# Attention in compact chunks whose scores contract over one head's 64 rows, with whole loads of queries and paired half loads on two queues

## The chip, the cores and the metric

The kernel runs on one core of one Trainium2 chip. The metric is the device time of one execution in microseconds (us), as the median of several runs; less is better. TensorE is called PE below, its weight loads PEld, VectorE DVE, ScalarE ACT, GpSimd POOL and SyncE SP.

## What is computed

Attention over 2 batches, 8 heads, 576 positions, 64 elements a head (float32). Heads 0 to 3 see a local window of 32 positions, heads 4 to 7 every 32nd position. Its result, as 1152 tokens of 512, goes through two products and a gated one, and then through four experts.

```python
stride = 32
scale = 1.0 / np.sqrt(D)
scores = scale * np.matmul(q, k.transpose(0, 1, 3, 2))
rel = pos[:, None] - pos[None, :]
mask_local = (rel >= 0) & (rel < stride)
mask_strided = (rel >= 0) & (pos[None, :] % stride == pos[:, None] % stride)
# masked scores, softmax over the keys, and the sum over v
x = attn_out.transpose(0, 2, 1, 3).reshape(B * S, H * D)   # 1152 x 512
a, b = x @ w1, x @ w2                                       # 512 -> 1024
x = ((a * b) @ w3) @ w_out                                  # 1024 -> 1024 -> 512
# four experts: out += p[:, e] * (relu(x @ w1[e]) @ w2[e])
```

## The kernel before

Attention output is kept as two float32r parts, `x_hi` and `x_lo` (value and remainder), and every large product is three matmuls of such parts (`mm3`). The float64 weights come as 1 MB loads (`raw`, two buffers) and are turned into the two parts by a chain of elementwise steps for each 128x1024 chunk: `round_up` (L121, ACT), `magnitude` (L127 DVE for the first chunk, L129 ACT for the others), `clamp` (L132), `shift` (L135), `sign` (L138) and `add` (L142) on DVE, then `split_hi` (L149, ACT) and `split_lo` (L159, DVE). A generator, `work()`, holds these steps for all chunks in one order; `advance(n)` issues the next n of them, and `need(c)` issues steps until chunk c is ready. `add` also issues the load of the raw chunk after next. A chunk is split only while `live`, the count of 128x1024 buffers in use (16 in all), is at most 14.

Attention runs in 22 tiles, 11 a batch: six of 96 queries for the four local heads, five of 126 or 108 for the strided ones (there queries are laid out by residue, 18 positions each). A tile takes: a mask matmul and four score matmuls into one bank (L285, L288; the queries of the other head of a pair are zeros, so that 128 rows are contracted), the maxima and their scaling (DVE, L294, L296), four exponentials with sums (ACT, L303), the division (DVE, L309, L310, L312), four transposes (L318), their evacuation in halves by ACT and DVE (L323), four value matmuls (L331), and `x_hi` (ACT, L345) and `x_lo` (DVE, L348).

The order is the program's own: every engine runs its instructions as the Python code issued them. The main loop is a pipeline over the tiles: step s holds the scores of tile s, the division of tile s-1, the transposes of tile s-3 and the values of tile s-4. From step 15 on, when the first batch (b = 0) is through, each step also issues one unit, `ab_block` (L232 to L234): 24 matmuls of 288 columns for one of 8 weight chunks `w12`, one batch and one half of its positions. There are 32 units, 16 of each batch. Units 2k and 2k+1 use chunk k, and batch 0's come first; chunk k's buffers come free with unit 17 + 2k. After unit 31 come `wc_tile` (`wc_acc`), `x3_block` and the experts; they are not touched by the change.

SP's queue carries nearly all loads in the order they are issued in; ACT's queue carries one. A DMA takes the next of eight semaphores (`DMAHW0` to `DMAHW7`) and waits until the DMA that held it before has landed; the wait stands in the program of the engine that issues it.

## Time and profile before

| | |
|---|---|
| median of 3 runs | 647.94 us (647.41 to 649.07) |
| the profiled execution, its time | 648.42 us |
| its span, first to last instruction | 646.6 us |
| PE / PEld / DVE / ACT busy, share of the span | 97% / 89% / 73% / 45% |
| first unit's first matmul | 48.57 us |
| first `wc` matmul, after all units | 167.83 us |

The span falls into three parts: attention of batch 0 up to 48.6 us, the units with what is left of attention up to 167.8 us, and the untouched rest. Busy shares are to be read stage by stage: PE's 97% holds long stretches at 100% and a start at about 75%. In the trace a float32 matmul stands as two passes (x8 is four matmuls), each with a weight load; the duration of a pass includes its way through the array, so the pace is read from start to start.

### The profile page before, as it was taken

The numbers are of one execution on the slowest core, as the hardware profiler recorded it, in microseconds if no ns is written. First come the engines' busy times: TensorE is split into PE (matmuls) and PEld (weight loads), VectorE is DVE, ScalarE is ACT, GpSimd is POOL, SyncE is SP. The second block draws the span as 40 slices with busy tenths as digits, with TensorE's granted clock in tenths as the row PEclk, the third lists the DMA queues.
The fourth block names the chain that finished last, engine by engine and source line by source line (L and its number), as shares of the span: only waits on it lengthen the run. The fifth ranks groups of instructions, "written<-read, shape, count | busy, mean of one in ns | idle before, by whom it ended". The sixth has DMA issues, their size and how long they took to land.

```text
span 646.6 us, 10360 instructions
## 1 busy us (share of the span) xinstructions
PE 629.1 (97%) x4052; PEld 572.7 (89%) x4052; DVE 470.6 (73%) x888; ACT 291.7 (45%) x628; POOL 6.9 (1%) x18
## 2 busy tenths in 40 slices
PE   7769999999999999999999999999999999999998
PEld 6659989999888999988999889988788989899896
DVE  8899999599875423777887787787776566665743
ACT  6787776466554323343333343344433333333321
POOL 4000000000000000000000000000000000000000
PEclk9989999999999999999999999999999999999999
DMA  8943133134433310234353355334478474656311
GB/s 227 308 133 131 66 131 131 67 131 143 183 131 130 131 66 1 67 131 188 137 188 138 134 192 183 142 131 163 163 260 322 151 247 153 228 177 239 130 66 66
DMA packets 26385, 98.73 MB, mean 153 GB/s; under 512 B 2528, under 2 KB 3808, under 8 KB 23776
## 3 DMA queue, kind: packets, MB, share of 16 engines
q1 hardware_dynamic: 26192, 97.97, 43.5%
q8 instruction: 32, 0.52, 0.4%
q14 instruction: 17, 0.14, 0.1%
q10 hardware_dynamic: 144, 0.10, 0.1%
HBM read 78.92 MB, written 19.14 MB: 152 GB/s over the span
## 4 chain that ended last, share of the span: by engine, by line
PE 85%; DVE 8%; DMA 3%; ACT 2%; SPq 1%; issue 1%; DVEq 0%
PE g_acc L233 10%; PE g_acc L234 10%; PE g_acc L232 10%; PE ab_acc L232 5%; PE ab_acc L234 4%; PE ab_acc L233 4%; PE m_a L232 4%; PE m_a L234 4%; PE m_a L233 4%; PE x_acc L232 3%; PE x_acc L233 3%; PE x_acc L234 3%; PE m_b L234 3%; PE m_c L232 3%; PE m_c L233 3%; PE m_c L234 3%
## 5 line engine op out<-in xcount | busy, mean ns | idle before, releaser
L517 ACT ACTIVATE h_hi<-u 128x320 fp32r<-128x320 f32 (+1 forms) x128 | 56.9, 445 | 189.2 <-DVE u L523 189.2
L233 PE MATMUL g_acc<-w_lo,h_hi 128*128 128x512 f32 (+1 forms) x296 | 114.9, 388 | 0.0
L232 PE MATMUL g_acc<-w_hi,h_hi 128*128 128x512 f32 (+1 forms) x296 | 114.7, 387 | 0.0
L234 PE MATMUL g_acc<-w_hi,h_lo 128*128 128x512 f32 (+1 forms) x296 | 114.6, 387 | 0.0
L523 DVE TENSOR_TENSOR u<-m_b,u 128x320 f32<-128x320 f32 (+1 forms) x96 | 40.8, 453 | 54.4 <-PE m_b L234 54.4
L456 DVE TENSOR_TENSOR w_lo<-raw,w_hi 128x768 fp32r<-128x768 f32 x64 | 69.4, 1085 | 12.0 <-ACT w_hi L454 11.9
L232 PE MATMUL ab_acc<-x_hi,w_hi 128*128 128x288 f32 x256 | 76.5, 299 | 0.0
L234 PE MATMUL ab_acc<-x_hi,w_lo 128*128 128x288 f32 x256 | 75.4, 295 | 0.0
L233 PE MATMUL ab_acc<-x_lo,w_hi 128*128 128x288 f32 x256 | 75.4, 294 | 0.0
L234 PEld LDWEIGHTS g_acc<-w_hi,h_lo 128*128 128x128 f32 x296 | 55.6, 188 | 12.2
L232 PEld LDWEIGHTS g_acc<-w_hi,h_hi 128*128 128x128 f32 x296 | 55.8, 189 | 8.6
L233 PEld LDWEIGHTS g_acc<-w_lo,h_hi 128*128 128x128 f32 x296 | 55.6, 188 | 8.4
L519 DVE SCALAR_TENSOR_TENSOR h_lo<-u,h_hi 128x320 fp32r<-128x320 f32 (+1 forms) x128 | 57.7, 451 | 3.5 <-ACT h_hi L517 1.4
L454 ACT CAST w_hi<-raw 128x768 fp32r<-128x768 f32 x64 | 59.9, 936 | 0.0
L232 PEld LDWEIGHTS ab_acc<-x_hi,w_hi 128*128 128x128 f32 x256 | 48.0, 187 | 1.5 <-issue 0.3
L233 PEld LDWEIGHTS ab_acc<-x_lo,w_hi 128*128 128x128 f32 x256 | 48.0, 188 | 0.0
L234 PEld LDWEIGHTS ab_acc<-x_hi,w_lo 128*128 128x128 f32 x256 | 48.0, 188 | 0.0
L303 ACT ACTIVATE p_pair<-sc,neg 96x128 f32<-96x128 f32 (+3 forms) x88 | 30.4, 355 | 18.5 <-DVE neg L296 17.3
L233 PE MATMUL m_b<-b_t,s_hi 128*128 128x320 f32 (+1 forms) x128 | 37.8, 295 | 0.0
L523 DVE TENSOR_TENSOR u<-m_a,u 128x320 f32<-128x320 f32 (+1 forms) x64 | 28.9, 452 | 11.8 <-PE m_a L234 11.8
L456 DVE TENSOR_TENSOR s_lo<-raw,s_hi 128x1024 fp32r<-128x1024 f32 x16 | 19.6, 1225 | 23.2 <-ACT s_hi L454 23.2
L121 ACT ACTIVATE raw<-raw 128x1024 int32<-128x1024 uint32 x20 | 23.5, 1174 | 27.4 <-DMA raw<-in_w3T_dram 19.5
(145 smaller groups left out, 1479.4 us busy)
## 6 DMA issues: line engine op xcount, KB each, us to landing
raw<-in_e_dram SPq DMA_DIRECT2D x32, 1024.0 KB, 5.2
raw<-in_w_dram SPq DMA_DIRECT2D x8, 1024.0 KB, 4.9
raw<-in_w3T_dram SPq DMA_DIRECT2D x8, 1024.0 KB, 4.8
stored<-s_hi SPq DMA_DIRECT2D x16, 512.0 KB, 2.6
stored<-s_lo SPq DMA_DIRECT2D x16, 512.0 KB, 2.6
s_hi<-stored SPq DMA_DIRECT2D x16, 512.0 KB, 4.7
s_lo<-stored SPq DMA_DIRECT2D x16, 512.0 KB, 6.2
raw<-in_w_out_dram SPq DMA_DIRECT2D x4, 1024.0 KB, 4.8
```

The lines of the kernel that those rows point to most:

```text
L121: nc.scalar.activation(self.low, self.low.bitcast(U32), AF.Copy, scale=2.0 ** -29)
L232: mm(acc, lh, rh, start=first, stop=False)
L233: mm(acc, lh, rl, start=False, stop=False)
L234: mm(acc, ll, rh, start=False, stop=last)
L303: nc.scalar.activation(self.p[:nq, h, :nk], self.sc[:nq, h, :nk], AF.Exp, bias=self.neg[:nq, h:h + 1], scale=SCALE, accum_out=self.sum[:nq ...
L454: nc.scalar.copy(dst[0], src)
L456: nc.vector.tensor_tensor(out=dst[1], in0=src, in1=dst[0].bitcast(F32), op=ALU.subtract)
L517: nc.scalar.activation(hi, src, AF.Relu)
L519: nc.vector.scalar_tensor_tensor(out=lo, in0=src, scalar=0.0, in1=hi.bitcast(F32), op0=ALU.max, op1=ALU.subtract)
L523: nc.vector.tensor_tensor(out=out, in0=acc, in1=b, op=ALU.add)
```

## The change

The diff below is cut. `tq` holds both heads of a pair and is loaded whole; scores contract over one head's 64 rows, on the half of the array where these rows lie, and nothing is set to zero first. Attention is cut into 6 chunks a batch instead of 11 tiles, class `Chunk4`.

A local chunk (g = 0, c = 0 to 2) has six blocks of 32 queries by 64 keys for each of four heads: one mask matmul over 384 columns and 24 score matmuls, each 32 weight columns by 64 moving columns, into one bank whose 128 partitions are four heads by 32 queries. Three transposes of 128x128 follow, and 24 value matmuls on the four quarters of the array (64 rows by 64 columns, 32 moving columns) into two banks. A strided chunk has four frames of up to 54 queries for four heads: a mask over 432 columns, 16 score matmuls, four transposes, 16 value matmuls.

On DVE a chunk takes a maximum and a subtraction over all columns, then a sum, the addition of 1e-9, the reciprocal, and the division; on ACT one exponential over all columns, one evacuation of 384 or 512 columns, and two to four casts to `x_hi`; DVE takes as many subtractions to `x_lo`.

The first load of queries and keys is cut at 288 positions. For batch 0 the keys go on SP's queue and the queries on ACT's, values and half loads alternate between both; ACT issues eight DMAs instead of one. The second group of batch 1 (`load_qk(1, 1)`, `load_v_str(1)`) is loaded after batch 0's attention. The first raw weight chunk moves ahead of most values in the order of issue. The loop is split: nine steps `attend(0, s)` for batch 0, with 18 extra dummy matmuls of 256 columns and two `advance` from step 4 on, then units, with `attend(1, s)` after units 2, 4, 5, 7, 8, 10, 11, 13 and 14 (counted from 1). `live` starts at 10, and a chunk gives back one buffer.

```diff
+T3 = 3 * NB
+CUT = 288
...
+    i_loc = const.tile([P, 4, W], BF16, name="i_loc")
+    i_str = const.tile([P, 2, 2 * W], BF16, name="i_str")
+    m_loc = const.tile([P, 7, 2 * W], BF16, name="m_loc")
+    m_str = const.tile([P, 3, NB], BF16, name="m_str")
...
-            mm(acc[:, :2 * P], zeros[:, :P], zeros, start=i == 0, stop=i == WARM - 1)
+
+        def keep_warm(n):
+            if n:
+                acc = bank("idle")
+            for i in range(n):
+                mm(acc[:, :2 * P], zeros[:, :P], zeros, start=i == 0, stop=i == n - 1)
+
+        keep_warm(WARM)
+        return keep_warm
...
-    live = 8
+    live = 10
...
+    def load_qk(b, g, cut=0):
+
+        tq, tk = (big[b].tile([P, 2, S], F32, tag="big", name=name) for name in ("tq", "tk"))
...
         for c in ([slice(0, cut), slice(cut, S)] if cut else [slice(0, S)]):
...
+            for t, src, queue in ((tk, kT, nc.sync), (tq, qT, nc.scalar if b == 0 else nc.sync)):
+                queue.dma_start(out=t[:, :, c], in_=src[b, pairs, :, c].rearrange("k p n -> p k n"))
+        qk[b, g] = (tq, tk)
...
+    def load_v_loc(b, c):
+
+        tv = wp.tile([P, 2, 3, P], F32, tag="w", name="tv_loc")
+
+        def load(dst, rows, t0, n, queue=nc.sync):
+            queue.dma_start(out=dst, in_=v_loc[b, :, rows, t0:t0 + n].rearrange("k p t d -> p k t d"))
...
+        lower, upper, middle = slice(0, 64), slice(64, P), slice(W, 3 * W)
+        other = nc.scalar if b == 0 else nc.sync
+        if c == 0:
+            load(tv[lower, :, 0:1], lower, 0, 1)
+            load(tv[upper, :, 0:1], middle, 0, 1, other)
+            load(tv[:, :, 1:], slice(0, P), 1, 2)
+        elif c == 1:
+            load(tv, slice(0, P), 3, 3)
+        else:
+            load(tv[lower, :, 0:1], lower, 0, 1)
+            load(tv[upper], middle, 3, 3, other)
+            load(tv[lower, :, 1:], middle, 1, 2)
+        vals[b, 0, c] = tv
+
+    def load_v_str(b):
+
+        threes = [wp.tile([P, n, P], F32, tag="w", name="tv_str") for n in (8, 4)]
+        queues = [nc.sync, nc.scalar if b == 0 else nc.sync]
+        for tv, t0, n in ((threes[0], 0, 4), (threes[1], 4, 1)):
+            for k, queue in enumerate(queues):
+                queue.dma_start(out=tv[64 * k:64 * k + T3, :2 * n].rearrange("p (h t) d -> p h t d", h=2),
+                                in_=v_str[b, k, :2 * T3, t0:t0 + n].rearrange("(h p) t d -> p h t d", h=2))
+        for k, queue in enumerate(queues):
+            queue.dma_start(out=threes[1][64 * k:64 * k + NB, 2:], in_=v_str[b, k, 2 * T3:2 * T3 + NB, :2])
+        vals[b, 1] = threes
...
+                if c < 2:
+                    self.groups = [(RS[t][0] + 3 * h, 3, 0, 4 * h + t) for t in (2 * c, 2 * c + 1) for h in range(2)]
+                else:
+                    self.groups = [(RS[4][0] + 3 * h, 3, 1, h) for h in range(2)]
+                    self.groups += [(RS[t][0] + 6, 1, 1, 2 + t) for t in range(2)]
+                self.frames, self.nk = 4, T3
+            self.slots = 2 * self.frames
...
         def scores(self):
...
+            tq, tk = qk[self.b, self.g]
+            bank = ps_sc.tile([P, 512], F32, tag="sc", name="sc")
+            self.sc = bank[:, :self.slots * self.nk].rearrange("p (s c) -> p s c", s=self.slots)
+            if self.g == 0:
+                mask = m_loc[:, :6] if self.c == 0 else m_loc[:, 1:]
+                mm(self.sc, flat(i_loc), mask, start=True, stop=False)
+                for s, i in enumerate(self.blocks):
+                    k0 = max(i - 1, 0) * W
+                    for h in range(4):
+                        r = slice(64 * (h % 2), 64 * (h % 2) + 64)
+                        mm(self.sc[32 * h:32 * h + 32, s], tq[r, h // 2, W * i:W * i + W],
+                           tk[r, h // 2, k0:k0 + 2 * W], start=False, stop=s == 5)
+            else:
+                mask = flat(m_str).unsqueeze(1).to_broadcast([P, self.slots, T3])
+                mm(self.sc, flat(i_str), mask, start=True, stop=False)
+                for f, (r, n, _, _) in reversed(list(enumerate(self.groups))):
+                    n = NB * n
+                    c = slice(NB * r, NB * r + n)
+                    for k in range(2):
+                        for j in range(2):
+                            r = slice(64 * j, 64 * j + 64)
+                            mm(self.sc[64 * j:64 * j + n, 2 * f + k, :n], tq[r, k, c], tk[r, k, c],
+                               start=False, stop=f == 0 and k == 1)
...
         def maxima(self):
...
+            s = self.slots
+            mx = small.tile([P, 8], F32, tag="mx", name="mx")
+            nc.vector.tensor_reduce(out=mx[:, :s], in_=self.sc, axis=mybir.AxisListType.X, op=ALU.max)
+            self.frame = p_ring[self.index % 4]
...
+            nc.vector.tensor_tensor(out=self.p, in0=self.sc, in1=self.wide(mx), op=ALU.subtract)
...
+            nc.scalar.activation(self.p, self.p, AF.Exp, scale=SCALE)
+
+        def sums(self):
+            s = self.slots
+            self.rec = small.tile([P, 8], F32, tag="rec", name="rec")
+            rec = self.rec[:, :s]
+            nc.vector.tensor_reduce(out=rec, in_=self.p, axis=mybir.AxisListType.X, op=ALU.add)
+            nc.vector.tensor_scalar_add(rec, rec, 1e-9)
+            nc.vector.reciprocal(rec, rec)
...
+            nc.vector.tensor_tensor(out=self.p, in0=self.p, in1=self.wide(self.rec), op=ALU.mult)
...
+            self.tp = bank("tp")[:, :self.frames * P]
+            for f in range(self.frames):
+                nc.tensor.transpose(self.tp[:, f * P:f * P + P], flat(self.frame[:, 2 * f:2 * f + 2]), ident)
+
+        def evac(self, copy):
+            n = self.frames * P
+            self.pT = tmp.tile([P, 512], F32, tag="pT", name="pT")[:, :n]
+            copy(self.pT, self.tp)
...
+            banks = [bank("o") for _ in range(2)]
+            if self.g == 0:
+                tv = vals[self.b, 0, self.c]
+                self.o = [o[:, :6 * W].rearrange("p (k f q) -> p k f q", k=2, f=3) for o in banks]
+                pT = self.pT.rearrange("p (f k j q) -> p f k j q", f=3, k=2, j=2)
+                todo = [(f, k, h, j) for f in range(3) for k in range(2) for h in range(2) for j in range(2)]
+                for f, k, h, j in todo:
+                    r, d = slice(64 * h, 64 * h + 64), slice(64 * j, 64 * j + 64)
+                    mm(self.o[h][d, k, f], tv[r, k, f, d], pT[r, f, k, j], start=True, stop=True)
...
+                for f, (_, n, i, at) in enumerate(self.groups):
+                    n = NB * n
+                    for h in range(2):
+                        for j in range(2):
+                            r, d = slice(64 * h, 64 * h + n), slice(64 * j, 64 * j + 64)
+                            mm(self.o[h][d, f, :n], vals[self.b, 1][i][r, at, d], pT[r, f, j, :n], start=True, stop=True)
...
+            self.ends = list(self.puts())
+            for o, (hi, _) in self.ends:
+                nc.scalar.copy(hi, o)
...
         def put_lo(self):
...
+            for o, (hi, lo) in self.ends:
+                nc.vector.tensor_tensor(out=lo, in0=o, in1=hi.bitcast(F32), op=ALU.subtract)
...
-        warm_up()
-        load_group(0, 0, nc.vector, 2 * QL)
-        constants()
-        load_group(0, 1, nc.vector)
-        load_next()
-        load_next()
-        load_group(1, 0, nc.gpsimd)
-        load_group(1, 1, nc.gpsimd)
+        keep_warm = warm_up()
+        load_qk(0, 0, CUT)
+        local_masks()
...
-            pair = big[1].tile([P, 2, 4, P], F32, tag="big", name="p_pair")
+            pair = big[1].tile([P, 2, 8, 2 * W], F32, tag="big", name="p_pair")
+            nc.gpsimd.memset(pair.rearrange("p a s c -> p (a s) c")[:, :, T3:], 0.0)
             p_ring += [pair[:, 0], pair[:, 1]]
-        tiles = [Tile(i, *bgt) for i, bgt in enumerate(
-            (b, g, t) for b in range(B) for g in range(2) for t in range((NL, len(RS))[g]))]
-        n = len(tiles)
+        make_identity(nc, ident)
+        strided_masks()
+        load_v_loc(0, 0)
+        load_qk(0, 1)
+        load_next()
+        load_v_loc(0, 1)
+        load_v_loc(0, 2)
+        load_v_str(0)
+        load_next()
+        load_qk(1, 0)
+        for c in range(3):
+            load_v_loc(1, c)
+        chunks = [[Chunk4(3 * g + c, b, g, c) for g in range(2) for c in range(3)] for b in range(B)]
         units = [(b, ft, i) for b in range(B) for ft in range(8) for i in range(2)]
...
-        first = n // 2 + 4
-        for s in range(n + 4):
...
+
+            nonlocal live
+            chunk = chunks[b]
+            n = len(chunk)
...
+                chunk[s].exps()
+                if b == 0:
+                    keep_warm({0: 6, 1: 4, 2: 4, 3: 4}.get(s, 0))
...
-                advance(1)
+                chunk[s - 1].sums()
+                chunk[s - 1].normalise()
+            if 2 <= s < n + 2:
+                chunk[s - 2].transposes()
+                chunk[s - 2].evac(nc.scalar.copy)
+            if 3 <= s:
+                c = chunk[s - 3]
+                c.pv()
+                c.put()
+                c.put_lo()
+                if c.g == 0 or c.c > 0:
+                    live -= 1
+
+        for s in range(9):
+            attend(0, s)
+            if s > 3:
+                advance(2)
+        load_qk(1, 1)
+        load_v_str(1)
+        steps = iter(range(9))
         while done < 16:
             run_unit()
+            if done in (2, 4, 5, 7, 8, 10, 11, 13, 14):
+                attend(1, next(steps))
         load_probs()
         while done < 32:
             run_unit()
```

ACT at the start of the program, before, with the semaphores that each row waits for (`p_pair` are the probabilities):

```order
L102 ACT_TABLE_LOAD
L102 ACTIVATE one<-idle 128x1 [waits DVE_49]
L254 DMA tq<-in_qT_dram 64x2x192
L303 ACTIVATE p_pair,sum<-sc,neg 96x96 [waits DVE_49,PE_49]
L303 ACTIVATE p_pair,sum<-sc,neg 96x96 x3
```

ACT at the same place after the change (`tv_loc` and `tv_str` are values of local and strided heads):

```order
L111 ACT_TABLE_LOAD
L111 ACTIVATE one<-idle 128x1 [waits DVE_49]
L262 DMA tq<-in_qT_dram 128x2x288 x2
L270 DMA tv_loc<-in_v_loc_dram 64x2x128
L262 DMA tq<-in_qT_dram 128x2x576 [waits DMAHW0_49]
L270 DMA tv_loc<-in_v_loc_dram 64x2x384 [waits DMAHW3_49]
L292 DMA tv_str<-in_v_str_dram 54x2x512 [waits DMAHW5_49]
L292 DMA tv_str<-in_v_str_dram 54x2x128 [waits DMAHW0_49]
L295 DMA tv_str<-in_v_str_dram 18x256 [waits DMAHW1_49]
L356 ACTIVATE p_pair<-p_pair 128x384 [waits DVE_49] x3
```

Seven more DMAs now stand ahead of the first exponential, five of them with a wait. `DMAHW1` was held by the second half of the keys and then by the first raw weight chunk, both on SP's queue; the program's last wait there is for the second of these.

ACT where the first batch's attention ends, before, with buffer numbers (`raw64_546` is the third raw weight chunk, the cast after it the last strided tile of batch 0):

```order
L121 ACTIVATE raw64_546<-raw64_546 128x1024
L323 COPY pT_673<-tp_668 96x2x96
L345 CAST x_hi_92<-o_676 128x2x6x18
L303 ACTIVATE p_pair_228,sum_683<-sc_655,neg_661 96x128 x4
L129 ACTIVATE t_688<-raw64_546 128x1024
```

ACT at the same place after the change (`raw64_596` is the third raw weight chunk, the casts after it are the last chunk of batch 0):

```order
L377 COPY pT_607<-tp_602 128x512
L425 CAST x_hi_93<-o_609 128x12x18
L425 CAST x_hi_93<-o_610 128x12x18
L136 ACTIVATE raw64_596<-raw64_596 128x1024
L425 CAST x_hi_93<-o_635 128x6x18
L425 CAST x_hi_93<-o_635 128x2x18
L425 CAST x_hi_93<-o_636 128x6x18
L425 CAST x_hi_93<-o_636 128x2x18
```

In both programs the third chunk's `round_up` stands ahead of batch 0's last `x_hi`. The load of that chunk is issued when the first chunk's `add` is done.

ACT where batch 1's attention ends, before, with buffer numbers (`o_1352` is the last tile; the last `w_hi` row is the seventh of the eight chunks `w12`):

```order
L345 CAST x_hi_92<-o_1307 128x2x6x18
L369 CAST ab_hi_1261<-ab_1263 128x288
L365 COPY ab_1315<-ab_acc_1316 128x288
L121 ACTIVATE raw64_1243<-raw64_1243 128x1024
L129 ACTIVATE t_1347<-raw64_1243 128x1024
L345 CAST x_hi_92<-o_1352 128x2x6x18
L369 CAST ab_hi_1261<-ab_1315 128x288
L365 COPY ab_1360<-ab_acc_1361 128x288
L149 CAST w_hi_1375<-t_1240 128x1024
```

ACT at the same place after the change (`o_1559`, `o_1560` are the last chunk; `w_hi_1585` is the eighth chunk of `w12`; `ab_acc_1593` belongs to unit 14, the first that uses it):

```order
L425 CAST x_hi_93<-o_1559 128x6x18
L425 CAST x_hi_93<-o_1559 128x2x18
L425 CAST x_hi_93<-o_1560 128x6x18
L425 CAST x_hi_93<-o_1560 128x2x18
L164 CAST w_hi_1585<-t_1269 128x1024
L450 CAST ab_hi_1467<-ab_1529 128x288
L446 COPY ab_1592<-ab_acc_1593 128x288
```

The eighth chunk's split now stands between the end of batch 1's attention and unit 14.

## Rows read from the trace of the kernel before

**Rows 1.** Busy time by stretch: start:end, length, busy (instructions), PEclk, DMA share, GB/s.

```profile
42.50:44.40 1.90, 0.00 (x0) 0.00 (x0) 1.80 (x7) 1.24 (x7) 0.00 (x0) 1.00 0.00 0
45.10:48.40 3.30, 3.30 (x21) 2.82 (x19) 3.20 (x8) 2.79 (x12) 0.00 (x0) 0.50 0.00 0
48.50:100.00 51.50, 50.95 (x431) 47.71 (x428) 49.94 (x104) 39.03 (x112) 0.00 (x0) 1.00 0.30 103
...
100.00:168.00 68.00, 67.99 (x514) 67.75 (x512) 9.36 (x21) 8.41 (x21) 1.00 0.37 129
```

**Rows 2.** Timeline of PE: start us, us, what; the first unit and the first `wc`.

```profile
48.57 0.40 PE L232 MATMUL ab_acc<-x_hi,w_hi 128*128 128x288 f32 x1
...
167.83 0.39 PE L232 MATMUL wc_acc<-w_hi 128*128 128x512 f32 x1
```

**Rows 3.** The chain that ended last, in order of time: start us, us, what.

```profile
8.80 12.93 DMA raw<-in_w_dram
...
24.77 0.60 DVE t L132
...
30.47 1.13 DVE t L138
...
64.33 1.22 DVE w_lo L159
```

**Rows 4.** Timeline of SP's and ACT's queues: DMA issues.

```profile
1.04 0.72 ACTq L254 DMA_DIRECT2D tq<-in_qT_dram  x1
...
11.36 0.38 SPq L251 DMA_DIRECT2D tk<-in_kT_dram  x1
14.86 2.38 SPq L254 DMA_DIRECT2D tq<-in_qT_dram  x2
```

**Rows 5.** Busy time by stretch, as in rows 1: the first 18 us.

```profile
0.00:18.00 18.00, 13.39 (x100) 10.35 (x100) 14.74 (x37) 11.31 (x55) 6.92 (x18) 1.00 0.89 243
```

**Rows 6.** Timeline of DVE: single steps of attention.

```profile
6.32 0.55 DVE L294 TENSOR_REDUCE neg<-sc 96x4 f32<-96x384 f32 x1
...
10.46 0.17 DVE L310 RECIPROCAL rec<-rec 96x4 f32<-96x4 f32 x1
...
47.99 0.54 DVE L348 TENSOR_TENSOR x_lo<-o,x_hi 128x216 fp32r<-128x216 f32 x1
...
51.63 0.34 DVE L348 TENSOR_TENSOR x_lo<-o,x_hi 128x192 fp32r<-128x192 f32 x1
```

**Rows 7.** DMA issues by line: KB each, median us from issue to landing.

```profile
raw<-in_w_dram SPq DMA_DIRECT2D x8, 1024.0 KB, 4.9
```

**Rows 8.** Timeline of ACT: a rounding, a split.

```profile
44.54 1.15 ACT L121 ACTIVATE raw<-raw 128x1024 int32<-128x1024 uint32 x1
...
52.15 1.05 ACT L149 CAST w_hi<-t 128x1024 fp32r<-128x1024 f32 x1
```

**Rows 9.** Timeline of PE: scores, transposes and values between two units.

```profile
57.13 0.38 PE L285 MATMUL sc<-m_str,ident_b 126*126 126x504 bf16 x1
57.35 1.04 PE L288 MATMUL sc<-tk,tq 128*126 128x126 f32 x8
58.23 0.50 PE L318 MATMUL tp<-ident,p_pair 96*128 96x96 f32 x4
58.65 0.55 PE L331 MATMUL o<-pT,tv 128*64 128x96 f32 x8
59.13 0.40 PE L232 MATMUL ab_acc<-x_hi,w_hi 128*128 128x288 f32 x1
```

**Rows 10.** Timeline of PE: values alone between matmuls of a unit.

```profile
97.01 0.29 PE L234 MATMUL ab_acc<-x_hi,w_lo 128*128 128x288 f32 x1
97.24 0.59 PE L331 MATMUL o<-pT,tv 108*64 108x108 f32 x8
97.76 0.40 PE L232 MATMUL ab_acc<-x_hi,w_hi 128*128 128x288 f32 x1
98.00 0.30 PE L233 MATMUL ab_acc<-x_lo,w_hi 128*128 128x288 f32 x1
```

More of the change, by code (lines that the diff above doesn't have):

```diff
@@ L103, in warm_up @@
         zeros = idle.bitcast(BF16)
-        acc = bank("idle")
-        for i in range(WARM):
-            mm(acc[:, :2 * P], zeros[:, :P], zeros, start=i == 0, stop=i == WARM - 1)
+        def keep_warm(n):
[5 more added lines that the diff above has]
+        return keep_warm
     class Chunk:
@@ L347, in put_lo @@
         def put_lo(self):
-            nc.vector.tensor_tensor(out=self.x[1], in0=self.o, in1=self.x[0].bitcast(F32), op=ALU.subtract)
+            for o, (hi, lo) in self.ends:
+                nc.vector.tensor_tensor(out=lo, in0=o, in1=hi.bitcast(F32), op=ALU.subtract)
     ab_hi, ab_lo = {}, {}
```

165 lines of the change are left out of this document (50 added, 115 removed).

## The prediction

> **What bounds the kernel now.** I read the stretches first, then PE's first unit and first `wc`, then the chain, the queues, and the single steps. From 100 us on PE is full: 514 unit matmuls in 68.0 us, 0.132 us each, 3.17 us a unit [rows 1]. From 48.5 to 100 us PE and DVE are both nearly full, 50.95 and 49.94 of 51.5 us [rows 1]. Before the first unit at 48.57 us [rows 2] PE has gaps, and the chain runs through the first raw weights (issued at 8.80 us, landed 12.93 us later) and from there over DVE [rows 3]. Nothing after 167.83 us [rows 2] is touched, so I forecast the start of `wc` alone and shift the end with it. That start is made of three parts: T, where the first unit can run; 32 units, 768 x 0.132 = 101.6 us; and what stands between units. Before it is 167.83 - 48.57 - 101.6 = 17.7 us of attention and gaps.
>
> **The start: ACT's queue.** ACT issues its loads itself, in its program's order [rows 4]. The change puts seven more ahead of the first exponential; the last waits for the first raw chunk to land. A queue does stand still on such a wait: after its issue at 11.36 us SP's next comes at 14.86 us [rows 4]. So the first exponential cannot run before that landing. What lands before it: on SP's queue 0.59 MB of keys, 0.33 of values, 0.59 of keys and the chunk's 1.05, on ACT's up to 1.66 MB, together up to 4.2 MB. The trace moved 243 GB/s over the first 18 us, 4.37 MB [rows 5], so 4.2 MB take to 17.4 us; if only 3.7 MB are ahead, to about 15.5. I take 18.0 us for the exponential, with 0.6 us for receipt and the issue behind it. Without the wait it could run at about 8 (an estimate: the first 0.59 MB of keys and queries are there a little after 5, scores, maximum and subtraction take the rest).
>
> **The start: DVE.** A reduction over 384 columns takes 0.55 us [rows 6]; the four passes of a local chunk 2.2, with two small steps of 0.17 [rows 6] 2.54; a strided chunk over 432 columns about 0.60 a pass, 2.74 (an estimate by columns). Six chunks: 3 x 2.54 + 3 x 2.74 = 15.8. Subtractions to `x_lo`: 0.30 for 192 plain columns (0.34 busy, overlapping the next), 0.54 for 216 strided ones [rows 6], about 0.3 for 108: local 3 x 0.6, strided 1.2 + 1.1 + 0.9, together 5.0. Weights up to the first unit: magnitude, two clamps and two shifts of about 0.6, three steps of 1.13, one of 1.22 [rows 3]: 7.7 with the first at 0.69. Sum 28.5, of which two chunks' maxima and subtractions (2.2) run while ACT waits. From 18.5 (one exponential, about 0.45) DVE would end at 18.5 + 26.3 = 44.8 us.
>
> Something later ends last: the third raw chunk can only be issued when the first chunk's `add` is done, 5.5 us before that end, at 39.3. Its 1 MB lands 4.9 us later [rows 7], 44.2; its `round_up` stands ahead of the last chunk's casts on ACT: 1.15 [rows 8], then four casts of 0.2 to 0.3 (an estimate from the subtractions' rows), and the last subtraction: 46.6 us. Only rows 2 and 3 of `x_hi` wait for it; the unit's first six matmuls (0.8 us) can run before. T is 45.8 in effect, 2.8 less than 48.57. The loads themselves are hidden: the weights of chunk two and batch 1 have no user that early. The masks on POOL end before the first scores need them; if not, they only use up time in which ACT waits. What is removed, zeroing `tq`, 22 scalings of maxima and 88 exponentials, is DVE and ACT work that had ended in this sum already.
>
> **The start: the clock.** PE has nothing to do between its last values, near 39 us, and T. Before, 1.9 us without a matmul [rows 1] were followed by a granted clock at half its full 2.4 GHz from 45.1 to 48.4 us, while PE was full; that was over when the first unit began. So 3.4 us of units at half pace now fall after T: +1.7 us, up to double.
>
> **Attention between units.** Of the new passes no row shows the size. Eight score passes of 126 columns take 58.23 - 57.35 = 0.88 us [rows 9], 0.110 each, one after the other; eight value passes of 96 columns on two column halves take 0.48 (58.65 to 59.13), 0.060 each, where one after the other they would take about 0.084. So two tiles of the array run side by side. By columns a pass of 64 takes 0.056 alone, 54 take 0.047, 32 take 0.028. A local chunk has 48 + 48 passes, a strided one 32 + 32. Low end, 0.014 a pass (four quarters side by side); high end, 0.060 (the value row's pace holds whatever the width). I take 0.024, half the pace alone, since two side by side is what the row shows. To it come the mask, 0.22, transposes at 0.105 each (58.23 to 58.65 is four), and the changes of tile shape: around the values the steps are 0.23 and 0.24 instead of 0.13 [rows 10], 0.2 for one group, two groups a chunk, say 0.5 in all. Local: 96 x 0.024 + 0.22 + 0.32 + 0.5 = 3.35. Strided: 64 x 0.024 + 0.22 + 0.43 + 0.5 = 2.7. Six chunks: 18.1 us, +0.4 against 17.7. At 0.014 it is 13.3, at 0.060 35. DVE has, from T to unit 14, six chunks (20.8), 28 products and remainders of units (about 0.41 each, 11.5) and seven chunks of weights (4.7 each with two already begun, 31): 63 us, against PE's 14 x 3.17 + 18.1 + 1.7 = 64. So DVE does not end later as a whole.
>
> **The eighth weight chunk.** `live` starts at 10; after batch 0 it is 5 and six chunks bring it over 14. Counted through, the eighth chunk's split is let in only when the last chunk of batch 1 has given back its buffer, after unit 13, and unit 14 needs it. PE waits for four casts (about 1.0 with 0.25 for the values to come out), the split's first part 1.05 and second 1.22 [rows 8, 3]: +3.5 us. Before, batch 1 was through ahead of unit 10, and the split stood among the units between. This wait is longer than the one that halved the clock [rows 1], so I count a second +1.7.
>
> **The sum.** -2.8 + 1.7 + 0.4 + 3.5 + 1.7 = +4.5 us. Against the profiled execution's 648.42 us this is 652.9; that execution lies 0.48 over the median, so 652.4 us.
>
> **Rivals.** First, ACT isn't held by its loads (the waits are served beside its instructions). Then the exponential runs at 8, DVE's 28.5 us and two to three us of waits for values end near 38, the third raw chunk lands at 37.3, and T is about 39 in effect: -9.6 + 1.7 + 0.4 + 3.5 + 1.7 = -2.3, 645.6 us. Against it speaks SP's standstill; for it, that no row shows ACT's queue with a wait.
>
> Second, faster: the array takes four quarters side by side, 0.014 a pass (-4.8), the raw chunk lands at 15.5 (-1.8), and the second wait leaves the clock alone (-1.7): 644.1 us. For it speaks that the two column halves overlap already [rows 9].
>
> Third, slower still: score passes on the two row halves do not run side by side, because all go into one bank. Then 48 passes at 0.056 and 32 at 0.047 instead of 0.024: +1.5 and +0.7 a chunk, +6.8 us in all, 659.2 us; it decides from 0.035 a pass on. The trace has column tiles alone, so nothing speaks against it. The Trainium skill, "TensorEngine Tiling (Array Packing)", section "Restrictions and Gotchas", says that different row tiles cannot access the same PSUM bank at once. By that rule the time is this rival's; by the trace [rows 9] it stays open, and no run here shows it yet.
>
> Fourth, between: half of the second's gains come, 648 us.
>
> **How the numbers follow.** About 0.3%, 1.9 us, can be told from no change here. The forecast as summed has 0.52, the first rival 0.10, the second 0.13, the third 0.15, the fourth 0.10. Of the forecast 0.05 reaches into no change (raw chunk early or no second clock loss), of the second nothing does. Faster 0.23, same 0.15, slower 0.62. The range is 644.0 to 659.0: it holds the forecast, the first and fourth rivals, half of the second and of the third. The forecast's own range is 649.5 to 657.
>
> **What would show it.** After the change: the first `p_pair` on ACT right behind the landing of the first raw chunk, near 18 us; DVE idle from about 10 to 18.5; the first unit near 46, with ACT waiting for the third raw chunk ahead of the last casts; a half clock after it; local scores of 1.1 us; PE idle 3.5 us ahead of unit 14; `wc` at 172.3 us. It is wrong if the exponentials start near 8, or if a chunk takes PE under 2.4 or over 4.5 us.

## The result, and the profile after

The changed kernel takes 651.95 us, the median of 12 runs (649.34 to 656.23), the kernel before 647.92 (12 runs, 646.35 to 649.37): a ratio of 1.0063, 95% interval 1.0044 to 1.0082. It is slower by about 4 us. The forecast was 652.4. The profiled execution took 651.43 us, its span is 649.6.

ACT and its queue after the change (timeline: start us, us, what; in brackets the idle time before it and what ended it) answer to [rows 4, 8]. The three `raw` rows are the third, the fourth and the fifth weight chunk.

```profile
7.71 5.86 ACTq L292 DMA_DIRECT2D tv_str<-in_v_str_dram  x2
15.76 0.29 ACTq L295 DMA_DIRECT2D tv_str<-in_v_str_dram  x1
16.10 0.94 ACT L356 ACTIVATE p_pair<-p_pair 128x384 f32<-128x384 f32 x2 [13.87 <-DMA raw<-in_w_dram]
...
43.92 1.19 ACT L136 ACTIVATE raw<-raw 128x1024 int32<-128x1024 uint32 x1 [2.67 <-DMA raw<-in_w_dram]
...
52.38 1.17 ACT L136 ACTIVATE raw<-raw 128x1024 int32<-128x1024 uint32 x1 [3.58 <-DMA raw<-in_w_dram]
...
62.27 1.12 ACT L136 ACTIVATE raw<-raw 128x1024 int32<-128x1024 uint32 x1 [4.12 <-DMA raw<-in_w_dram]
```

The first exponential stands behind ACT's last load and that load behind the first raw weights. PE after the change answers to [rows 2, 9, 10]: the first unit's k = 2 matmul, two transposes between units, the last values of batch 1, two matmuls of unit 14, and the first `wc`.

```profile
45.45 0.61 PE L247 MATMUL ab_acc<-x_hi,w_hi 128*128 128x288 f32 x1 [1.06 <-ACT x_hi L425]
...
68.36 0.55 PE L372 MATMUL tp<-ident,p_pair 128*128 128x128 f32 x3 [1.80 <-DVE p_pair L367]
...
83.31 0.52 PE L372 MATMUL tp<-ident,p_pair 128*128 128x128 f32 x3 [0.86 <-DVE p_pair L367]
...
110.19 0.81 PE L398 MATMUL o<-pT,tv_str 54*64 54x54 f32 x32
112.60 0.40 PE L247 MATMUL ab_acc<-x_hi,w_hi 128*128 128x288 f32 x1 [1.61 <-ACT w_hi L164]
...
114.08 0.40 PE L249 MATMUL ab_acc<-x_hi,w_lo 128*128 128x288 f32 x1 [0.95 <-DVE w_lo L174]
...
172.70 0.39 PE L247 MATMUL wc_acc<-w_hi 128*128 128x512 f32 x1
```

`wc` starts 4.87 us later than before [rows 2]; 4.5 were forecast. The span is only 3.0 longer: the rest took 478.8 us before and 476.9 after, though the matmuls are the same in both: up to 272 us `wc` and what follows lie 4.87 us later, from there on, in the experts, the lead of the kernel before shrinks evenly to 2.9. In the twelve kernels below, the rest took 476.4 to 477.7. Why the one execution of before was slower there stays open; nothing of it is laid to the change.

Busy time by stretch after the change (columns as in [rows 1]; the third pair is DVE):

```profile
0.00:6.40 6.40, 4.89 (x64) 3.44 (x65) 0.17 (x1) 1.49 (x2) 4.24 (x19) 1.00 0.72 226
6.40:16.60 10.20, 3.75 (x112) 2.64 (x111) 2.23 (x4) 0.50 (x2) 0.00 (x0) 0.82 1.03 320
16.60:45.00 28.40, 18.12 (x370) 14.17 (x370) 24.86 (x53) 13.57 (x30) 0.00 (x0) 0.68 0.57 176
45.00:70.00 25.00, 22.75 (x274) 21.46 (x275) 20.22 (x34) 13.78 (x25) 0.00 (x0) 0.89 0.62 198
70.00:114.03 44.03, 40.02 (x567) 36.67 (x566) 41.59 (x85) 26.38 (x56) 0.00 (x0) 1.00 0.28 97
...
0.00:114.03 114.03, 89.54 (x1384) 78.38 (x1384) 89.06 (x175) 55.72 (x111) 4.24 (x19) 0.88 0.52 166
...
115.00:120.00 5.00, 5.00 (x29) 5.00 (x28) 2.43 (x4) 2.90 (x4) 0.00 (x0) 0.66 0.00 0
```

The same view of the kernel before, over its start and up to the end of the eighth chunk's `w_lo`:

```profile
0.00:6.30 6.30, 4.22 (x24) 3.07 (x25) 4.24 (x5) 1.49 (x2) 5.19 (x17) 1.00 0.63 161
...
0.00:110.32 110.32, 97.80 (x810) 86.67 (x811) 102.69 (x227) 81.67 (x274) 6.92 (x18) 0.98 0.53 162
```

The account below goes by DVE, and the runs support it as far as its idle time goes; no run tests what less work on DVE would be worth. Both stretches from 0 end with `w_lo` of chunk eight, at 110.32 and 114.03 us. Until then DVE worked 102.7 us before and 89.1 after: the change does take 13.6 us of work off DVE. But DVE was idle for 7.6 us before and for 25.0 after, 17.3 more. In the first 6.4 us it is idle for 6.2 (2.1 before, when it zeroed `tq` beside the first loads, so 4.1 of the saved work lay where DVE has to wait for the first scores anyway); from 6.4 to 16.6 for 8.0, nearly all of it for the exponential; from 45 to 70 for 4.8, half of it behind weights that come late (1.91 behind the fifth chunk's `round_up`, 0.52 behind the fourth's) and the rest in gaps of 0.5 us or less. DVE's waits for the exponential and for the fifth chunk (timeline):

```profile
16.65 0.55 DVE L362 TENSOR_REDUCE rec<-p_pair 128x6 f32<-128x384 f32 x1 [7.34 <-ACT p_pair L356]
...
63.74 0.46 DVE L452 TENSOR_TENSOR ab_lo<-ab,ab_hi 128x288 fp32r<-128x288 f32 x1 [1.91 <-ACT ab_hi L450]
```

From `w_lo` to `wc` stand 57.5 us before and 58.7 after, with a half clock from 115 us on (0.66 from 115 to 120).

### The profile page after: what moved, and what is told of

It is laid out like the page before. It is cut to its first block, busy times and chain, and to the rows that moved or that the text cites. A ratio compares the mean times of both kernels' runs of the same rounds, so it can differ in the third digit from the quotient of the medians.

```text
span 649.6 us, 11313 instructions
## 1 busy us (share of the span) xinstructions
PE 620.0 (95%) x4622; PEld 565.8 (87%) x4622; DVE 456.1 (70%) x834; ACT 265.0 (41%) x464; POOL 4.2 (1%) x19
## 4 chain that ended last, share of the span: by engine, by line
PE 82%; DMA 7%; DVE 7%; ACT 2%; issue 2%; SPq 0%; ACTq 0%; DVEq 0%
PE g_acc L247 10%; PE g_acc L248 10%; PE g_acc L249 9%; DMA raw<-in_w_dram 5%; PE m_a L247 4%; PE m_a L249 4%; PE m_a L248 4%; PE ab_acc L249 4%; PE ab_acc L247 4%; PE ab_acc L248 3%; PE x_acc L249 3%; PE x_acc L247 3%; PE x_acc L248 3%; PE m_b L249 3%; PE m_c L247 2%; PE m_b L248 2%
## 5 line engine op out<-in xcount | busy, mean ns | idle before, releaser
L247 PE MATMUL ab_acc<-x_hi,w_hi 128*128 128x288 f32 x256 | 78.9, 308 | 3.0 <-ACT w_hi L164 1.6
L249 PE MATMUL ab_acc<-x_hi,w_lo 128*128 128x288 f32 x256 | 77.6, 303 | 1.4 <-DVE w_lo L174 1.4
L248 PE MATMUL ab_acc<-x_lo,w_hi 128*128 128x288 f32 x256 | 77.4, 302 | 0.0
L247 PEld LDWEIGHTS ab_acc<-x_hi,w_hi 128*128 128x128 f32 x256 | 49.9, 195 | 4.3 <-ACT w_hi L164 1.7
L249 PEld LDWEIGHTS ab_acc<-x_hi,w_lo 128*128 128x128 f32 x256 | 49.8, 194 | 2.0 <-DVE w_lo L174 2.0
L248 PEld LDWEIGHTS ab_acc<-x_lo,w_hi 128*128 128x128 f32 x256 | 49.9, 195 | 0.2 <-DVE x_lo L429 0.2
L136 ACT ACTIVATE raw<-raw 128x1024 int32<-128x1024 uint32 x20 | 23.2, 1161 | 36.5 <-DMA raw<-in_w3T_dram 20.5
L537 DVE TENSOR_TENSOR s_lo<-raw,s_hi 128x1024 fp32r<-128x1024 f32 x16 | 19.6, 1225 | 23.2 <-ACT s_hi L535 23.2
L604 DVE TENSOR_TENSOR u<-m_c,u 128x320 f32<-128x320 f32 (+1 forms) x64 | 28.9, 452 | 4.5 <-PE m_c L249 3.8
```

Of the source, the lines that this page charges most:

```text
L136: nc.scalar.activation(self.low, self.low.bitcast(U32), AF.Copy, scale=2.0 ** -29)
L247: mm(acc, lh, rh, start=first, stop=False)
L248: mm(acc, lh, rl, start=False, stop=False)
L249: mm(acc, ll, rh, start=False, stop=last)
L537: nc.vector.tensor_tensor(out=dst[1], in0=src, in1=dst[0].bitcast(F32), op=ALU.subtract)
L604: nc.vector.tensor_tensor(out=out, in0=acc, in1=b, op=ALU.add)
```

## The experiments

`wc` is the start of the first `wc` matmul. DVE's busy and idle time is counted up to the end of `w_lo` of chunk eight, or of the last `x_lo` where that is later (marked *). Ratios are to the kernel before, with the 95% interval.

| | median us | ratio | wc us | DVE busy | DVE idle |
|---|---|---|---|---|---|
| changed kernel | 651.95 | 1.0063 [1.0044, 1.0082] | 172.70 | 89.1 | 25.0 |
| e1_act_free | 642.28 | 0.9926 [0.9903, 0.9949] | 163.88 | 88.5 | 16.7 |
| e2_raw_after_values | 650.15 | 1.0038 [1.0020, 1.0055] | 172.15 | 89.0 | 24.5 |
| e3_buffers | 663.53 | 1.0247 [1.0226, 1.0268] | 185.21 | 91.6* | 37.0* |
| e4_warm | 652.82 | 1.0081 [1.0057, 1.0105] | 173.20 | 89.0 | 24.7 |
| e5_strided_buffers | 652.12 | 1.0066 [1.0046, 1.0085] | 173.95 | 91.7* | 25.6* |
| e7_round_up_later | 653.63 | 1.0083 [1.0058, 1.0108] | 176.38 | 88.9 | 27.6 |
| e6_act_and_buffers | 642.38 | 0.9916 [0.9888, 0.9945] | 166.32 | 91.2* | 17.1* |
| e8_all_three | 642.44 | 0.9912 [0.9882, 0.9942] | 164.02 | 91.0* | 16.4* |
| e9_group_early | 648.68 | 1.0013 [0.9998, 1.0029] | 170.34 | 88.7 | 23.2 |
| e10_act_free_group_early | 647.28 | 0.9979 [0.9963, 0.9995] | 169.35 | 88.4 | 21.2 |
| e12_group_between | 642.08 | 0.9902 [0.9883, 0.9920] | 164.93 | 88.4 | 17.1 |
| e11_ab_lo_pool | 653.90 | 1.0088 [1.0060, 1.0115] | 174.79 | 88.7 | 26.5 |

The `wc` and DVE columns are of one execution, the profiled one. DVE's work is the same within 0.7 us in every row without a mark, and `wc` follows its idle time. Busy and idle time add up to the end of DVE's step by construction, so the table alone doesn't show that DVE sets the pace. Two kinds of run speak for it: where DVE's idle time is taken away, `wc` follows (e1_act_free, e9_group_early), and where a loss of PE alone is taken away, it doesn't (e4_warm, e5_strided_buffers).

### ACT's loads

**e1_act_free** takes the five loads that carry a wait off ACT's queue.

```diff
-for t, src, queue in ((tk, kT, nc.sync), (tq, qT, nc.scalar if b == 0 else nc.sync)):
+for t, src, queue in ((tk, kT, nc.sync), (tq, qT, nc.scalar if b == g == 0 else nc.sync)):
-other = nc.scalar if b == 0 else nc.sync
+other = nc.scalar if b == c == 0 else nc.sync
-queues = [nc.sync, nc.scalar if b == 0 else nc.sync]
+queues = [nc.sync, nc.sync]
```

> The changed kernel with five of ACT's loads (those that carry a semaphore wait) moved to SP's queue; ACT keeps three loads without a wait. Theory 1 (ACT's program is held by its loads until the first raw weights have landed): the first exponential starts near 8.5 us instead of 16.10, ACT no longer has the idle stretch of 13.9 us ended by the raw load, the first unit's k = 2 matmul comes near 39.5 us instead of 45.45, wc starts near 167 us instead of 172.70, time near 646.5 us. Theory 2 (the wait only covers something that ends as late, the weights or the values): the exponential is early, but the k = 2 matmul stays within 1.5 us of 45.45, wc at 171.5 or later, time 651 us.

Measured: 642.28 us. ACT's first exponential, PE's k = 2 matmul and first `wc`, and busy time up to the end of the eighth chunk's `w_lo`:

```profile
7.91 0.52 ACT L356 ACTIVATE p_pair<-p_pair 128x384 f32<-128x384 f32 x1 [5.67 <-DVE p_pair L350]
```

```profile
36.97 0.61 PE L247 MATMUL ab_acc<-x_hi,w_hi 128*128 128x288 f32 x1 [0.99 <-ACT x_hi L425]
...
163.88 0.39 PE L247 MATMUL wc_acc<-w_hi 128*128 128x512 f32 x1
```

```profile
0.00:105.19 105.19, 88.10 (x1384) 76.87 (x1384) 88.54 (x175) 55.80 (x111) 4.26 (x19) 0.92 0.55 180
```

Theory 1 holds, and by more than it expected: 8.8 us at `wc`, where 5.7 were expected. DVE's idle time fell by 8.3. The edit also puts five more loads on SP's queue, so the gain is that of both together. This version beats both kernels: with ACT free, the rest of the change is worth about 5 us against the kernel before (ratio 0.9926).

**e2_raw_after_values** moves the first `load_next()` behind `load_v_str(0)`.

> The changed kernel with the first raw weight load moved behind all values of batch 0 in the order of issue; ACT's loads stay on ACT, but the last wait ahead of its exponential is now for a value load. Theory 1 (the exponential waits for whatever load ACT's last wait names): the first exponential starts near 12 us instead of 16.10, the first raw chunk lands some 2 us later than 15.7, the first unit's k = 2 matmul comes near 42 us, wc near 169.5 us, time near 648.7 us. Theory 2 (it is the bytes moved ahead of it, or the weights' landing sets the first unit): the exponential stays near 16, wc within 1 us of 172.70, time 652 us.

Measured: 650.15 us. ACT's first exponential:

```profile
13.83 0.94 ACT L356 ACTIVATE p_pair<-p_pair 128x384 f32<-128x384 f32 x2 [11.60 <-DMA tv_str<-in_v_str_dram]
```

The wait is now for a value load, and the exponential is 2.3 us sooner. `wc` gained only 0.55: DVE's wait for the exponential fell from 7.3 to 3.7 us, its waits for scores grew by 2.4, and its idle time in all fell by 0.5. So the hold of ACT's queue is shown, but the size expected of this edit (3.2 us at `wc`) was wrong. That early raw weights help or harm by themselves isn't settled by it.

### The clock and the wait ahead of unit 14

**e4_warm** adds dummy matmuls in steps 5 to 8 of batch 0.

```diff
+if b == 0:
+    keep_warm({5: 10, 6: 12, 7: 12, 8: 12}.get(s, 0))
```

> The changed kernel with 46 more dummy matmuls of 256 columns in the last four steps of batch 0's attention. Theory 1 (the half clock from 33.4 to 50.5 us costs half of the 5.0 us that lie behind the first unit's k = 2 matmul): the clock is full there, units run at 3.2 us from the start, wc 2.0 to 2.6 us earlier than 172.70, time near 649.5 us. Theory 2 (DVE sets the pace up to 100 us, so a faster PE only waits for it): full clock, but wc within 0.8 us of 172.70, time 651.5 us. Theory 3 (the dummies themselves delay transposes and values on PE): the first unit later, wc at 173 us or more.

Measured: 652.82 us. Busy time by stretch (the granted clock is the third number from the end), then PE's longest wait between units:

```profile
33.00:50.00 17.00, 13.07 (x178) 10.96 (x177) 14.37 (x26) 9.15 (x19) 0.00 (x0) 1.00 0.30 93
```

```profile
68.06 0.90 PE L372 MATMUL tp<-ident,p_pair 128*128 128x128 f32 x3 [3.80 <-DVE p_pair L367]
```

In the changed kernel the same stretch had a clock of 0.51. At full clock PE came sooner to the transposes and waited there 3.80 us instead of 1.80; `wc` is 0.5 later. Theory 2 holds: the half clock after the first unit, 2.5 us of PE's time, cost nothing. The time would fit theory 3 as well, but its cause doesn't: the first unit's k = 2 matmul ran at 45.19, no later than the 45.45 of the changed kernel.

**e3_buffers** was meant to free buffers for the eighth chunk by putting three value tiles of batch 1 into `big[1]`; it had room for two.

> The changed kernel with three value tiles of batch 1 placed in tiles that lie empty until unit 16, so that the eighth weight chunk's split needs no buffer of the last attention chunk; nothing else changes. Theory 1 (the wait ahead of unit 14 and the half clock behind it are lost time): no PE idle of about 2.6 us between 110 and 114 us, no half clock at 115 us, wc starts 3 to 4.6 us earlier than 172.70, time near 648 us. Theory 2 (DVE has no room before unit 14, the split's work only displaces attention): new PE waits for DVE between 50 and 110 us eat most of it, wc 0 to 1.5 us earlier, time 651 us.

Measured: 663.53 us (ratio 1.0247, 1.0226 to 1.0268). The wait of SP's queue, and PE's wait that came of it:

```profile
SPq L294 <- PE sc L332: 16.4, 1, 16.4
```

```profile
80.10 0.90 PE L374 MATMUL tp<-ident,p_pair 128*128 128x128 f32 x3 [12.39 <-DVE p_pair L369]
```

The third tile's load had to wait on SP's queue until batch 1's scores had read the tile that it replaces. The raw weight loads stood behind it, DVE behind them, and PE 12.39 us behind DVE. It says nothing on unit 14, but shows what one waiting load on a queue does.

**e5_strided_buffers** does it with the two strided tiles alone.

```diff
-threes = [wp.tile([P, n, P], F32, tag="w", name="tv_str") for n in (8, 4)]
+pool, tag = (big[1], "big") if b == 1 else (wp, "w")
+threes = [pool.tile([P, n, P], F32, tag=tag, name="tv_str") for n in (8, 4)]
-live = 10
+live = 8
-if c.g == 0 or c.c > 0:
+if c.g == 0 or b == 0 and c.c > 0:
```

> The changed kernel with the two strided value tiles of batch 1, and only these, placed in the two tiles that lie empty until unit 16 (in e3_buffers a third tile had to wait for one in use); live starts at 8 and batch 1 gives back its three local tiles, so that the seventh and eighth weight chunks are split two units earlier. Theory 1 (the wait ahead of unit 14 and the half clock behind it are lost time): no PE idle of 2.6 us ahead of unit 14, no half clock behind it, wc starts 3 to 4.6 us earlier than 172.70, time near 648.5 us. Theory 2 (DVE has no room before unit 14, so the splits displace attention there): PE waits for DVE between units grow by 2 us or more, wc 0 to 1.5 us earlier, time 651 us.

Measured: 652.12 us. PE at the last values of batch 1:

```profile
113.34 0.32 PE L399 MATMUL o<-pT,tv_str 54*64 54x54 f32 x4 [1.09 <-ACT pT L378]
...
114.34 0.79 PE L399 MATMUL o<-pT,tv_str 54*64 54x54 f32 x28 [0.67 <-DVE x_lo L430]
```

The wait ahead of unit 14 is gone: the eighth chunk was ready at 108.99 us. The attention that DVE did not get to in that time now waits instead, and its last `x_lo` ends at 117.35. PE's other waits from unit 1 on, for DVE and ACT, grew from 3.3 to 5.6 us, so theory 2 holds as to the cause; its `wc` does not, which was to come no later than 172.70 and came at 173.95. Which of the two is late is a matter of order; that DVE has both to do before unit 14 is through is what costs. A half clock followed here too (0.66 from 115 to 120 us, as in the changed kernel), so the run doesn't show what that second clock loss costs.

**e7_round_up_later** issues one step fewer after step 7 and one more after step 8, `advance({7: 1, 8: 3}.get(s, 2))`.

> The changed kernel with the third raw chunk's round_up and the sign step beside it issued behind the last x_hi casts and x_lo subtractions of batch 0 instead of ahead of them. Theory 1 (that wait of 2.67 us and the step of 1.19 us on ACT set the first unit's k = 2 matmul, and PE's start carries through to wc): the k = 2 matmul at about 43.3 us instead of 45.45, right behind the weights' w_lo at 43.06, wc 1.5 to 2.1 us earlier than 172.70, time near 650 us. Theory 2 (DVE's sum of work up to unit 14 decides, as the run with dummies says): the k = 2 matmul as early, but the wait at the transposes between units grows by as much, wc within 0.6 us of 172.70, time 651.7 us.

Measured: 653.63 us. PE at the first unit and at the transposes:

```profile
43.79 0.61 PE L249 MATMUL ab_acc<-x_hi,w_lo 128*128 128x288 f32 x1 [0.43 <-DVE w_lo L174]
...
70.94 0.90 PE L372 MATMUL tp<-ident,p_pair 128*128 128x128 f32 x3 [6.27 <-DVE p_pair L367]
```

The first unit runs through from 43.79, but PE waits 6.27 us at the transposes. Here the fifth chunk's `round_up` came at 64.87 instead of 62.27, though its load was issued at 54.20 (53.93 before the edit). Theory 2 was right that nothing is gained. The later `wc` was expected by neither theory, and why the load took 2 us longer stays open. It is shown by one execution, the slowest of six (654.57 us); over all of them the ratio's interval overlaps that of the changed kernel, so a loss isn't shown.

**e6_act_and_buffers** and **e8_all_three** add these edits to e1_act_free.

> The edits of e1_act_free and of e5_strided_buffers together. Theory 1 (the two losses add up, since they lie in different stretches): wc at about 160.5 us, time near 639 us. Theory 2 (what the start gains is DVE's debt later: with attention done sooner, DVE sets the pace up to unit 14): wc within 1.5 us of e1_act_free's 163.9, time near 642 us.

> The edits of e1_act_free, e5_strided_buffers and e7_round_up_later together. If the losses add up: wc near 158.7 us, time near 637.3 us. If DVE decides between the units: the same as e6_act_and_buffers within 0.6 us.

Measured: 642.38 us (0.9916, 0.9888 to 0.9945) and 642.44 (0.9912, 0.9882 to 0.9942), the same as e1_act_free. Neither the buffers nor the order are worth anything there. The `wc` of e6_act_and_buffers, 2.4 us later than in e1_act_free, is that of an execution of 644.52 us, 2.1 over its median.

### The loads of batch 1's second group

**e9_group_early** loads the group at the start, as the kernel before did.

```diff
         load_v_loc(1, c)
+    load_qk(1, 1)
+    load_v_str(1)
...
-    load_qk(1, 1)
-    load_v_str(1)
     steps = iter(range(9))
```

> The changed kernel with one part undone: batch 1's second group (queries, keys and strided values, 1.7 MB) is loaded at the start behind the other loads, as the kernel before did, and not between the fourth and fifth raw weight chunks. Theory 1 (these bytes keep the DMA engines full from 49 to 60 us, so the fifth chunk lands 8 us after its issue instead of 5, DVE stands idle for 4.8 of the 25 us from 45 to 70, and since it is full from 70 to 110 that idle time reaches wc): the fifth chunk's round_up near 59 us instead of 62.27, DVE idle there about 2 us, the 1.80 us wait at the transposes at 68 us gone, wc 2 to 4 us earlier than 172.70, time near 649 us. Theory 2 (the idle time of DVE is caught up later, or the early loads hold up the first chunks): wc within 0.6 us of 172.70 or later, time 652 us or more.

Measured: 648.68 us. ACT at the fifth chunk, and busy time by stretch:

```profile
58.74 1.16 ACT L136 ACTIVATE raw<-raw 128x1024 int32<-128x1024 uint32 x1
```

```profile
45.00:70.00 25.00, 24.03 (x288) 22.77 (x288) 22.53 (x38) 13.54 (x25) 0.00 (x0) 0.90 0.38 127
```

The fifth chunk is rounded at 58.74 with no wait (62.27 after 4.12 us of waiting in the changed kernel), DVE's idle time from 45 to 70 falls from 4.8 to 2.5, the 1.80 us wait at the transposes is gone, and `wc` is 2.36 sooner. Theory 1 holds.

**e10_act_free_group_early** and **e12_group_between** join it with e1_act_free; the second loads the group after step 6, behind the third raw chunk.

> The edits of e1_act_free and e9_group_early together. If both losses are real and apart: wc near 161 us (163.9 less 3), time near 639.5 us. If the start, 8.5 us sooner, finds the queue still full of the early loads (DMA full to 31 us and beyond): the third raw chunk lands later than 35.5 us, wc at 164 or later, time 642.5 us or more.

> The edit of e1_act_free, and batch 1's second group loaded right behind the third raw weight chunk instead of behind the fourth (e10_act_free_group_early loaded it ahead of the third, which then landed some 7 us late). Theory 1 (the group's bytes cost only where a raw chunk that is waited for stands behind them): the first unit's k = 2 matmul stays near 37 us, the fifth chunk's round_up comes near 50.5 us instead of 53.43, DVE's idle time from 36 to 60 us (4.6 us in e1_act_free) falls to about 2, wc 2 to 3.5 us earlier than 163.9, time near 639.5 us. Theory 2 (the queue's semaphores or the fourth chunk take it back): the fourth chunk's round_up later than 43.9 us by 1 us or more, wc at 163.5 or later, time 642 us or more.

Measured: 647.28 us and 642.08 us. ACT at the third chunk in the first, and at the fourth in the second:

```profile
42.05 1.10 ACT L136 ACTIVATE raw<-raw 128x1024 int32<-128x1024 uint32 x1 [7.39 <-DMA raw<-in_w_dram]
```

```profile
46.43 1.16 ACT L136 ACTIVATE raw<-raw 128x1024 int32<-128x1024 uint32 x1 [4.15 <-DMA raw<-in_w_dram]
```

With ACT free the third chunk's load is wanted sooner, while the early group still fills the queue: it waited 7.39 us (2.63 in e1_act_free), and half the gain of e1_act_free went back. Behind the third chunk the group delays the fourth (43.90 in e1_act_free) and speeds the fifth (52.11 against 53.43); it comes out even. The second theory held both times.

### DVE's work

**e11_ab_lo_pool** moves the `ab_lo` subtraction of the first units to POOL (`engine = nc.gpsimd if done < 15 else nc.vector`).

> The changed kernel with the subtraction to ab_lo of the first units (0.37 us each on DVE, some 15 of them, 5.5 us) moved to POOL, which is idle; its result is read only after wc. Theory 1 (DVE's sum of work sets the time up to unit 14): the waits at the transposes (1.80 and 0.86 us) and ahead of unit 14 (2.6 us) shrink, wc 3 to 5 us earlier than 172.70, time near 648 us. Theory 2 (weights' landing and the fixed order decide, DVE's busy share only fills the waits; or POOL's work slows DVE's): wc within 1 us of 172.70, time 651 to 653 us.

Measured: 653.90 us (1.0088, 1.0060 to 1.0115), `wc` at 174.79, later than either theory has it; the ratio's interval overlaps that of the changed kernel. One subtraction on POOL, and DVE's step beside it:

```profile
74.44 0.82 POOL L453 TENSOR_TENSOR ab_lo<-ab,ab_hi 128x288 fp32r<-128x288 f32 x1 [5.58 <-ACT ab_hi L450]
```

```profile
74.50 1.84 DVE L157 CUSTOM_DVE_ANT_0 t<-raw,t 128x2048 uint16<-128x2048 uint16 x1
```

DVE's `add` takes 1.84 us beside POOL's step; DVE's groups between 70 and 110 us show its mean, here and in the changed kernel:

```profile
L157 DVE CUSTOM_DVE_ANT_0 t<-raw,t 128x2048 uint16<-128x2048 uint16 x4 | 6.5, 1631 | 0.0
```

```profile
L157 DVE CUSTOM_DVE_ANT_0 t<-raw,t 128x2048 uint16<-128x2048 uint16 x4 | 4.9, 1221 | 0.0
```

DVE's time up to `w_lo` of chunk eight stayed at 88.7 us although 13 of its instructions were gone. So the run doesn't test whether less DVE work brings `wc` forward; that was left open.

## Why the prediction was right, and which of its steps were not

The time and the sign were right, and so was ACT's hold, without which the kernel would have been faster (e1_act_free). The rest of the sum came out partly by luck. The terms, beside what the trace shows:

- **ACT's queue: right.** Expected at 18.0 us, the first exponential ran at 16.10; the loads moved faster than the 243 GB/s that were assumed (320 from 6.4 to 16.6 us). The first rival, ACT not held, fell: e1_act_free shows what it would have been. It put the gain of a free ACT at 6.8 us; 9.7 were measured, 8.8 of them at `wc`.
- **T: -2.8 forecast, -3.9 measured.** Six matmuls of 0.132 us before 45.45 make 44.66 in effect. The third raw chunk did end last, ahead of the last casts, as forecast.
- **The clock after T: +1.7 forecast, 2.5 measured as PE's time, and worth nothing** (e4_warm). The step "so 3.4 us of units at half pace now fall after T: +1.7" took PE for the engine that sets the end there. The half clock also began earlier than its step says, at 33.4 us and not after 39, when PE had been busy for only 0.57 us from 30 to 33.
- **Attention between units: +0.4 forecast, about -0.7 measured**, counting 172.70 - 44.66 - 101.6 = 26.4 less the clock (2.5 and 1.7), the transposes' waits (2.66) and unit 14's (2.56): 17.0 against 17.7, 2.8 a chunk. A value pass took 0.020 us at most (48 of them from 22.82 to 23.79, below), a strided score pass 0.029 with the change of shape; 0.024 was assumed.
- **"So DVE does not end later as a whole": the step that failed.** Its sum was nearly right: 63 us were forecast from T to unit 14, and DVE was busy for 61.8 from 45 to 114. It compared that with PE's 64 us and found room, but left out the time in which DVE has nothing to work on, 7.2 us in that stretch. Of this 4.8 lie from 45 to 70, half of them because the fourth and fifth raw chunks were waited for. Part of the cause is in the change: the second group's loads between the two. The prediction asked of batch 1's loads only who uses them ("have no user that early"), not what stands behind them. e9_group_early shows 2.4 us of it at `wc`. PE lost 1.80 us at the transposes for it; its other wait there, 0.86 us, stands in e9_group_early too (0.81).
- **The eighth chunk: +3.5 forecast, 2.56 of PE idle measured, and it is no cost of its own** (e5_strided_buffers). The second clock loss came, +1.7, behind it; what it costs no run shows by itself.

So +4.5 met +4.87 partly by luck: too much for attention and the eighth chunk, nothing for DVE's waits. Without the two terms that the runs show to be no cost, the first clock loss and the eighth chunk, the forecast's own sum would have been -0.7; DVE's idle time filled their place. Summed as DVE's time the account is shorter: 13.6 us of work gone, 17.3 us of idle time come, +3.7, and 1.2 behind `w_lo`, +4.9.

Of the second rival's gains, ACT's last load came as early as it said (issued at 15.76) and the local passes came part of the way (0.018 to 0.020 us); the second clock loss was there. The third rival fell. Here are PE's values, strided scores and transposes in the changed kernel, and one chunk's local scores (timeline; the granted clock is full in all but the first row, where it averages 0.82):

```profile
22.82 1.04 PE L389 MATMUL o<-pT,tv_loc 64*64 64x32 f32 x48
23.79 0.36 PE L334 MATMUL sc<-m_str,i_str 128*128 128x432 bf16 x1
24.08 1.01 PE L341 MATMUL sc<-tk,tq 64*54 64x54 f32 x32
25.01 0.55 PE L372 MATMUL tp<-ident,p_pair 128*128 128x128 f32 x3
25.49 0.89 PE L389 MATMUL o<-pT,tv_loc 64*64 64x32 f32 x44
27.63 0.30 PE L389 MATMUL o<-pT,tv_loc 64*64 64x32 f32 x4 [1.25 <-issue]
...
65.69 0.87 PE L330 MATMUL sc<-tk,tq 64*32 64x64 f32 x48
```

The 48 local score passes, which alternate between the two row halves and all go into one bank, took 0.87 us, under 0.019 each; one after the other they would take 0.056 (the prediction's estimate by columns). By the Trainium skill, "TensorEngine Tiling (Array Packing)", section "Restrictions and Gotchas", different row tiles cannot access the same PSUM bank at once. The trace does not agree: at 0.87 us for 48 the passes of the two halves do run side by side, and the measurement decides.

## To carry to other kernels

Where several engines are nearly full, add up the busiest one's work and its idle time to the point where its last result is needed, and ask of each edit which of the two it changes; PE's own waits and clock along the way need not cost anything. Only the idle time was tested here. A load put on the queue of an engine that also computes brings its semaphore waits into that engine's program, so only loads without a wait belong there. A load that has no user yet can still cost if it stands ahead of one that is waited for.

## What the runs showed of the hardware

- A POOL subtraction of 0.8 us makes DVE's step beside it longer by 0.5 to 0.6 where it starts first (1.84, 1.77 and 1.71 against 1.22 us). Where DVE's step starts first it keeps its time, and POOL's takes 1.26 us instead of 0.82, as in these rows of e11_ab_lo_pool (timelines of DVE and POOL):

```profile
106.92 1.21 DVE L157 CUSTOM_DVE_ANT_0 t<-raw,t 128x2048 uint16<-128x2048 uint16 x1
```

```profile
107.54 1.26 POOL L453 TENSOR_TENSOR ab_lo<-ab,ab_hi 128x288 fp32r<-128x288 f32 x1 [4.06 <-ACT ab_hi L450]
```

  The Trainium skill, "SBUF — State Buffer", section "SBUF: two separate sides", says that, for such a DVE step with two SBUF inputs, the two engines share one pair of ports as an exclusive lock, held for the whole instruction by the one that starts first. The rows agree in that the first one kept its time.
- PE stopped in the middle of 48 equal passes, after the 44th, with no releaser in the profile: 1.25 us in the changed kernel (row 27.63 above) and 3.37 us in e12_group_between, while the DMA engines were busy for 1.03 and 0.82 of the time. Ten of the thirteen kernels with such passes show it, with 0.22 to 3.37 us. PE's timeline in e12_group_between:

```profile
16.78 0.89 PE L389 MATMUL o<-pT,tv_loc 64*64 64x32 f32 x44 [0.46 <-DMA tv_loc<-in_v_loc_dram]
21.04 0.42 PE L389 MATMUL o<-pT,tv_loc 64*64 64x32 f32 x4 [3.37 <-issue]
```

  The Trainium skill, "Runtime: NRT & Kernel Launch", section "Instruction fetch mechanics", says that an engine's program is fetched by DMA block by block and that this is mostly hidden. A fetch held up behind loads would look like this; no run here tests it, so the cause stays open.
